# Sinkhorn-sorted attention with a bilinear FFN: output products of two batches and a sixth of batch 0's a, b products by Strassen blocks, in a fixed order of work

## The chip, the cores and the metric

The kernel runs on one core of a Trainium2 chip. The metric is the device time of one execution in microseconds (us), read as the median of several executions. The span in a profile runs from the first to the last instruction and is 1.8 to 2.2 us shorter than the device time. Engines are named as the profile names them: PE is TensorE (matmul), PEld its weight load, DVE is VectorE, ACT is ScalarE, POOL is GpSimd, SP is SyncE; "SPq" is a transfer issued from SP's queue.

## The reference, cut to what matters

```python
def _attn_ref(q, k, v, sort_net):              # q, k, v: 4 x 8 heads x 768 x 64; sort_net: 4 x 8 x 8 x 8
    P = sort_net
    for _ in range(5):                         # Sinkhorn
        P = np.exp(P - np.max(P, axis=-1, keepdims=True))
        P = P / (np.sum(P, axis=-1, keepdims=True) + 1e-09)
        P = P / (np.sum(P, axis=-2, keepdims=True) + 1e-09)
    k_sorted = np.einsum('bhij,bhjcd->bhicd', P, k_b)      # mixes the 8 blocks of 96 tokens
    v_sorted = np.einsum('bhij,bhjcd->bhicd', P, v_b)
    ...                                        # softmax attention inside each block of 96 tokens
def _moe_ref(x, w_a, w_b, w_out):              # x: 3072 x 512; w_a, w_b: 512 x 1536; w_out: 1536 x 512
    return (x @ w_a) * (x @ w_b) @ w_out
```

## The kernel before: the parts that matter

The kernel describes its work as a list of pieces (`add(engine, duration, function, deps, ...)`). A planner, run while the kernel is built, gives each piece a time and an engine by a greedy rule; then the instructions are emitted once, engine by engine, in the order of the plan. The emitted program holds, for each engine, that order and the semaphores to wait for, and no times.

Heads are worked on in *pairs*, four for each batch. The *spread* (`s_all<-mask,p_col`) writes the Sinkhorn result out as blocks for PE; a *mix* is a PE product of `s_all` with k or v. A *plain* product is one without Strassen blocks. *Warm-up* products (`warm_sb`; in the changed kernel `ps<-ws_b`) compute nothing that is used; they keep PE busy in the first 34 us.

The a, b products of batches 1 to 3 use Strassen blocks: seven block products for eight, at the price of sums of weight blocks (`ws_a`, `ws_b`, "w sums", 16 in all, done once) and of activation blocks (`tx`, "x sums", four for each batch). In this kernel all 16 go to GpSimd:

```python
    def w_sums(rank):
        oks = {}
        al = (("POOL", 1.75),)                       # engine and assumed us
        for n, w_sb, ws in (("a", w_a_sb, ws_a), ("b", w_b_sb, ws_b)):
            for c in range(2):
                ... # [cut: slices of w_sb and of ws]
                    op = add(al, None, None, dj, rank=rank)
                    op.fn = lambda ...: tt(op.eng, s[j], x, y, o)   # tensor_tensor

    last = o_p                                       # Sinkhorn, all 32 (batch, head) rows at once
    for it in range(5):
        ... # [cut: exp on ACT; on DVE row sum, reciprocal, p_nat *= 1/row, column sum, reciprocal, p_nat *= 1/column]

    def v_out(b, p):                                 # sorted v leaves to DRAM in one layout ...
        nc.sync.dma_start(out=vdram[b, p], in_=buf(("vb", b, p))...)
    def v_back(b, p):                                # ... and comes back in another, as vs
        nc.sync.dma_start(out=buf(("vs", b, p))[:, :, 2:2 + 2 * D], in_=_ap(vd, 0, ...))
```

The softmax here doesn't subtract the row's maximum and nothing guards it: scores larger than these inputs give would overflow.

## Time and profile before

The median is 245.03 us (244.59 to 245.09, four executions).

| | before |
|---|---|
| span, mean granted TensorE clock | 243.3 us, 1.00 |
| PE busy / DVE busy / POOL busy | 233.7 / 150.1 / 119.6 us |
| first plain a, b product | 27.46 us |
| start of the last matmul | 238.3 us |
| the 16 w sums on GpSimd | between 29 and 71 us, 1.65 us each |

The page's busy table of the kernel before, engine by engine (busy us, share of the span, instructions):

```profile
PE 233.7 (96%) x2204; PEld 132.4 (54%) x2204; DVE 150.1 (62%) x348; ACT 125.3 (52%) x243; POOL 119.6 (49%) x132
```

PE is the limit. The waits view of the kernel before, PE only (line, what it waited for, us in total, times, longest), shows what little it loses:

```profile
engine line waited for: us in total, times, longest us
PE ps L983 <- DVE warm_sb L326: 1.3, 1, 1.3
PE ps L473 <- DMA q<-in_q_dram: 1.1, 2, 0.6
PE ps L500 <- issue: 1.0, 1, 1.0
PE ps L593 <- ACT eT L583: 0.8, 1, 0.8
```

Two stretches of the kernel before, from the busy table by stretch (busy us and, in brackets, instructions of each engine; then clock, DMA share and GB/s):

```profile
core 0: us, PE busy (x) PEld busy (x) DVE busy (x) ACT busy (x) POOL busy (x), PEclk, DMA share, GB/s
50.00:60.00 10.00, 10.00 (x148) 6.75 (x144) 5.41 (x11) 7.66 (x13) 9.96 (x9) 1.00 1.24 194
60.00:70.00 10.00, 10.00 (x126) 6.14 (x124) 6.46 (x12) 5.99 (x10) 9.96 (x10) 1.00 1.00 148
```

Groups of w sums in the kernel before (count, busy us, mean ns, idle time before):

```profile
L306 POOL TENSOR_TENSOR ws_b<-w_b_sb 128x768 bf16<-128x768 bf16 x4 | 6.6, 1648 | 0.0
```

### The profile page before, as it was taken

The page shows a single profiled execution, that of the slowest core. Times are in us where ns is not written, and L with a number is a line of the kernel's source. Part 1 is how long each engine was busy: PE and PEld are TensorE (multiplying, and loading weights), DVE is VectorE, ACT ScalarE, POOL GpSimd, SP SyncE. Part 2 cuts the span into 40 slices and gives each one's busy share as a digit, 9 for nine tenths or more (in the row PEclk, how much of TensorE's full clock was granted, in tenths as well). Part 3 has the DMA queues.
Part 4 walks back from the last instruction along what each step waited for, and adds up shares of the span by engine and source line. Part 5 has one row for each costly group of instructions (what it writes and reads, how often), then busy time and mean ns, then how long its engine had stood idle before and what let it go on. Part 6 is the DMA issues. An engine that isn't in the chain of part 4 may idle for free.

```text
span 243.3 us, 5723 instructions
## 1 busy us (share of the span) xinstructions
PE 233.7 (96%) x2204; PEld 132.4 (54%) x2204; DVE 150.1 (62%) x348; ACT 125.3 (52%) x243; POOL 119.6 (49%) x132
## 2 busy tenths in 40 slices
PE   6998999999989999999999999999999999999992
PEld 2466766666655554665544455665654455565440
DVE  6656654654555738589987452988862448886210
ACT  3366646468655533667654443766631076673100
POOL 8979999999970020069755110173540007355000
PEclk9999999999999999999999999999999999999999
DMA  5999999999965683619998867200035450000135
GB/s 67 180 203 187 202 203 187 167 191 178 162 134 107 167 184 78 149 16 154 135 175 110 192 174 178 46 0 0 3 66 108 96 122 0 1 0 3 43 86 129
DMA packets 50106, 27.90 MB, mean 115 GB/s; under 512 B 28832, under 2 KB 47008, under 8 KB 50080
## 3 DMA queue, kind: packets, MB, share of 16 engines
q0 software_dynamic: 24112, 14.16, 43.3%
q1 hardware_dynamic: 25968, 13.38, 25.7%
q8 instruction: 17, 0.28, 0.5%
q14 instruction: 9, 0.07, 0.1%
HBM read 30.29 MB, written 8.26 MB: 158 GB/s over the span
## 4 chain that ended last, share of the span: by engine, by line
PE 67%; ACT 1%; DVE 1%; issue 0%; ACTq 0%; DVEq 0%
PE ps L831 33%; PE ps L899 26%; PE ps L593 2%; PE ps L578 2%; PE ps L489 1%; PE ps L537 1%; PE ps L473 1%; PE ps L749 1%; ACT f L840 0%; DVE xp L604 0%; ACT o L248 0%; DVE a L306 0%; DVE rec L599 0%; ACTq L840 0%; DVEq L306 0%
## 5 line engine op out<-in xcount | busy, mean ns | idle before, releaser
L306 POOL TENSOR_TENSOR hT<-a,f 128x384 bf16<-128x384 bf16 x39 | 35.5, 918 | 78.1 <-DVE f L306 56.3
L899 PE MATMUL ps<-w_out_sb,hT 128*128 128x512 bf16 x288 | 66.4, 379 | 0.0
L840 ACT COPY f<-ps 128x384 f32<-128x384 f32 x108 | 48.2, 482 | 23.6 <-PE ps L831 21.1
L899 PEld LDWEIGHTS <-hT 128*128 128x128 bf16 x288 | 27.0, 98 | 30.1
L306 DVE TENSOR_TENSOR a<-f,ps 128x384 bf16<-128x384 f32 x54 | 29.4, 549 | 10.4 <-PE ps L831 6.4
L306 DVE TENSOR_TENSOR f<-f,ps 128x384 f32<-128x384 f32 x54 | 28.9, 550 | 8.9 <-PE ps L831 6.0
L583 ACT ACTIVATE eT<-ps 96x768 bf16<-96x768 f32 x32 | 24.9, 806 | 17.2 <-PE ps L578 16.9
L306 DVE TENSOR_TENSOR hT<-a,ps 128x384 bf16<-128x384 bf16 x42 | 23.1, 551 | 12.4 <-PE ps L749 6.9
L248 ACT COPY o<-ps 128x512 f32<-128x512 f32 x15 | 8.8, 585 | 36.3 <-PE ps L899 36.3
L831 PE MATMUL ps<-tx,ws_a 128*128 128x384 bf16 x108 | 25.2, 326 | 0.2 <-ACT f L840 0.2
L831 PE MATMUL ps<-tx,ws_b 128*128 128x384 bf16 x108 | 24.9, 326 | 0.3 <-ACT f L840 0.3
L604 DVE TENSOR_TENSOR xp<-ps,rec 96x512 bf16<-96x512 f32 x32 | 21.4, 677 | 0.4
L749 PE MATMUL ps<-xT,w_a_sb 128*128 128x384 bf16 x96 | 19.6, 327 | 0.0
L749 PE MATMUL ps<-xT,w_b_sb 128*128 128x384 bf16 x96 | 19.6, 326 | 0.0
L831 PEld LDWEIGHTS <-ws_b 128*128 128x128 bf16 x144 | 13.8, 98 | 10.1 <-ACT f L840 0.9
L755 ACT CAST a<-ps 128x384 bf16<-128x384 f32 x24 | 11.5, 479 | 14.9 <-PE ps L749 9.1
L250 DVE COPY o<-ps 128x512 f32<-128x512 f32 x9 | 6.2, 691 | 20.8 <-PE ps L899 20.7
L831 PEld LDWEIGHTS <-ws_a 128*128 128x128 bf16 x144 | 13.5, 98 | 10.1 <-ACT f L840 1.4
L831 PE MATMUL ps<-xT,w_b_sb 128*128 128x384 bf16 x72 | 17.6, 326 | 0.3 <-DVE xp L604 0.2
L831 PE MATMUL ps<-xT,w_a_sb 128*128 128x384 bf16 x72 | 17.5, 326 | 0.0
L831 PEld LDWEIGHTS <-w_b_sb 128*128 128x128 bf16 x108 | 10.4, 98 | 7.9 <-DVE xp L604 0.7
L831 PEld LDWEIGHTS <-w_a_sb 128*128 128x128 bf16 x108 | 10.3, 98 | 7.9 <-ACT f L840 0.6
(90 smaller groups left out, 337.9 us busy)
## 6 DMA issues: line engine op xcount, KB each, us to landing
out_dram<-o SPq DMA_DIRECT2D x48, 128.0 KB, 2.4
k<-in_k_dram POOLq DMA_DIRECT2D x16, 192.0 KB, 6.1
v<-in_v_dram POOLq DMA_DIRECT2D x16, 192.0 KB, 6.1
vd<-vm SPq DMA_DIRECT2D x10, 192.0 KB, 2.9
vs<-vd SPq DMA_DIRECT2D x10, 192.0 KB, 3.1
q<-in_q_dram POOLq DMA_DIRECT2D x16, 96.0 KB, 6.9
w_a_sb<-in_moe_w_a_dram POOLq DMA_DIRECT2D x4, 384.0 KB, 7.1
w_b_sb<-in_moe_w_b_dram POOLq DMA_DIRECT2D x4, 384.0 KB, 9.0
```

Source lines behind the costliest of these rows:

```text
L248: nc.scalar.copy(out=out, in_=in_)
L250: eng.tensor_copy(out=out, in_=in_)
L306: ENG[eng].tensor_tensor(out=out, in0=in0, in1=in1, op=op)
L578: nc.tensor.matmul(sc[:, e, i * BLK:(i + 1) * BLK], lhsT=kT[e * D:(e + 1) * D, at:at + P], rhs=rhs, start=True, stop=True)
L583: nc.scalar.activation(out=buf(("eT", b, p, h))[:, :, 0:HB], in_=buf(("sc", b, p, h))[0:BLK, :, 0:HB], func=AF.Exp, scale=float(scale))
L593: nc.tensor.matmul(ops_[:, e, i * OW:(i + 1) * OW], lhsT=eT[:, e, i * BLK:i * BLK + P], rhs=vs[:, h * NBH + i, e * OW:(e + 1) * OW], start ...
L604: nc.vector.tensor_tensor(out=_ap(xp, h * NBH * 2 * D, [[NB * 2 * D, BLK], [D, 2], [2 * D, NBH], [1, D]]), in0=_ap(ops_, 2, [[1024, BLK], ...
L749: nc.tensor.matmul(pf[:, 0:HW], lhsT=w_sb[:, kc, m * P:(m + 1) * P], rhs=buf(("xT", b))[:, kc, t * HW:(t + 1) * HW], start=(kc == 0), stop ...
L755: ea = add("ACT", 0.48, lambda: nc.scalar.copy(out=buf(("a", b, t, m)), in_=buf(("pf", b, t, m, "a"))[:, 0:HW]), [pa], get=[("a", ("a", b, ...
L831: nc.tensor.matmul(buf(key)[:, 0:HW], lhsT=lf(j), rhs=rf(j), start=start and j == 0, stop=j == 1, skip_group_check=not start)
L840: return add("ACT", 0.48, lambda: nc.scalar.copy(out=buf((name, b, g, n)), in_=buf(kA)[:, 0:HW]), [dep], get=[("f", (name, b, g, n))], rank=r)
L899: nc.tensor.matmul(po, lhsT=hT[:, t * 2 + m // G, m % G, c * P:(c + 1) * P], rhs=w_out_sb[:, m, :], start=(m == 0), stop=(m == KO - 1), sk ...
```

## The change

It is meant to take work off PE and to start PE's products sooner:

- output products of batches 2 and 3 by Strassen blocks (252 products of 256 columns for 144 of 512), with 48 more sums of activations ("S sums") and 8 of weights;
- one sixth of batch 0's a, b products by Strassen blocks too, which needs batch 0's x sums and the w sums early;
- batch 0's Sinkhorn alone first, in another layout with small matmuls; that of batches 1 to 3 later, beside other work;
- w chunks loaded in the order 0, 2, 1, 3, and seven of the 16 w sums on VectorE;
- the order of all pieces from a fixed list in place of the greedy rule; in the plan, sums on GpSimd and VectorE that carry a `port` mark may not overlap.

```diff
+RATE = 365e3
+ORDER = ( b"-b&,###'#+#7#)... [cut: 37 lines, one choice of piece and engine for each two bytes]" )
-STRASSEN_OUT = ()
+STRASSEN_OUT = (2, 3)
+PLAIN_G = 5
...
+        def begin(op, e, w):                        # plan only: marked sums don't overlap
+            return max(at[e], w, port) if e in op.port else max(at[e], w)
...
-    for c in range(1, 4):
+    for c in (2, 1, 3):
         load_ab(c)
...
-        al = (("POOL", 1.75),)
-        for n, w_sb, ws in (("a", w_a_sb, ws_a), ("b", w_b_sb, ws_b)):
-            for c in range(2):
+        for c in (1, 0):
+            al = (("POOL", 1.75), ("DVE", 0.55)) if c == 1 else (("POOL", 1.75),)
+            for n, w_sb, ws in (("a", w_a_sb, ws_a), ("b", w_b_sb, ws_b)):
...
-                    op = add(al, None, None, dj, rank=rank)
+                    op = add(al, None, None, dj, rank=rank - 30.0 * c, port=("POOL", "DVE"))
...
+    if PLAIN_G < G:
+        tx_ok = x_sums(0, R0 + 30.0)
+        for g in range(PLAIN_G, G):
+            ab_strassen(0, g, R0 + 48.0 + 2.0 * (g - PLAIN_G), ws_ok, tx_ok, [])
... [cut: o_sums and out_strassen (about 145 lines), batch 0's Sinkhorn by matmuls, the planner's bookkeeping]
```

## The prediction

> **What bounds it.** TensorE. The page's busy table has PE at 233.7 us of a 243.3 us span; in the busy table by stretch PE is full from 27.46 us (first plain a,b product) to 238.7 us (0.96 us idle), granted clock 1.00. The tail is 4.6 us (last eviction 0.59, then the store). In the timeline, steps from matmul start to start are 163 ns (384 columns) and 216 ns (512): columns/2.4 GHz + 2.5 ns, as the Trainium skill says ("TensorE: Matmul & The Clock Gate", section "Wait — 56ns, not 53.3ns?"); they agree. Estimate for 256 columns: 109 ns; its 98 ns weight load should hide, as 128-column products step at 56 ns.
>
> **Before the first plain product.** Of the first 27.5 us, PE's real work is about 12.2 us (counts x mean step); the rest is warm-up and waits. The Sinkhorn chain (five iterations of 1.76 us, 2.29 to 11.05 us), copies and a spread queued behind warm-up matmuls put the first mix at 14.4 us; the first half of batch-0 attention then takes 13 us.
>
> **What the change does to PE work** (counts from the two instruction orders):
> - Output of batches 2 and 3 by Strassen: 144 x 216 ns = 31.2 us becomes 252 x 109 ns = 27.5 us: -3.7 us.
> - Batch 0: 32 plain products of 384 columns become 28: -0.65 us.
> - Batch-0 Sinkhorn by matmuls: six small f32 products, about +1.5 us (guess), where PE waits anyway.
>
> Added elsewhere: 48 S sums (DVE 0.33 estimated from 0.55 for 768 columns, POOL 0.92), 8 W sums, 4 x sums, more ACT snapshots. In the a,b stages DVE is 85% and POOL 42% busy, so these fit: a few tenths of us of new PE waits. The order is now a fixed list, so waits at 70.9 us (0.8 us) and in the batch-1 Strassen stage (0.3 us each) may go.
>
> **The start.** Only batch 0's Sinkhorn precedes the first mix: 1.6 us + 4 x about 1.45 us (ACT 0.26, PE, three DVE ops, hops) + 1 us: first mix near 11 us, not 14.4. But k of pair 3 now comes after w chunk 0 and two more q halves: 2.9 MB into SBUF; at before's landing rate, near 20.5 us (v of pair 3 landed at 15.5). About 5 us of attention follow: first plain product at about 25.7 us, with 14.6 us of real work done against 12.2. That gains about 1.8 + 2.4 - 1.5 = 2.7 us.
>
> **Tail.** Last piece is 256 columns (0.42 for 0.59-0.69 us), its two stores go to two queues: -0.5 us.
>
> **Sum.** 245.0 - 4.3 (products) - 2.7 (start) - 0.5 (tail) - 0.9 (fewer waits of the search) = 236.6 us. Range 233.8 to 239.6. Faster by over 2% (under 240.1): 0.92; within 2%: 0.07; slower: 0.01.
>
> **What would show each step.** 256-column steps at 109 ns; first mix at 10.5 to 11.5 us; PE waiting for k of pair 3 near 20 us; the last matmul at about 231 us; PE idle under 2 us between; output stages of batches 2 and 3 near 14 us instead of 15.9.
>
> **What would make it wrong.** The 256-column products bound by weight loads (+2 to 3 us); S sums on a slow POOL holding up the output stage (1 to 3 us each); DVE and POOL slowing each other; weight chunks late for the fixed order, stalling PE at 26 to 45 us; the other way, k landing earlier (-1.5 us).

## More of the kernel before

*Held* means that an instruction lasts longer than the shortest one of its form.

A w sum adds or subtracts two SBUF operands of 128x768.

All loads from the inputs are issued by GpSimd (`nc.gpsimd.dma_start`, they convert float32 to bfloat16); the read-back `vs<-vd` and the stores go out on SP's queue. So GpSimd has two jobs: issuing loads, and sums.

In the rounds of the later experiments this kernel's median was 245.1 to 245.6 us.

## The result

The changed kernel is correct and takes 262.25 us median (258.2 to 265.62, four executions); the ratio to the kernel before is 1.061 (95% interval 1.049 to 1.074). All ratios here are the mean time of one kernel's executions over that of the other's in the same rounds, so not quite the ratio of the medians quoted. Executions over 1.5% slower than the fastest of the same kernel are left out of the means. The prediction was 236.6 us, and "slower" had been given 0.01. The times of the changed kernel scatter; its profiled execution (265.62 us) is one of the two that count as slow for it, so the profile below overstates the time by some 2%. The clock goes with it, but only roughly: its four executions had mean granted clocks of 0.945, 0.973, 0.979 and 0.957 in the order 265.6, 262.8, 258.2 and 261.7 us. The explanation therefore rests on the experiments' executions, not on this profile alone.

The page's busy table of the changed kernel:

```profile
PE 239.0 (91%) x2306; PEld 147.3 (56%) x2306; DVE 187.3 (71%) x425; ACT 130.7 (50%) x264; POOL 148.4 (56%) x163
```

DVE is 37 us busier and POOL 29 us. PE's own busy time should have fallen by some 4 us and has risen. The waits view of the changed kernel, PE:

```profile
PE ps L900 <- DVE hT L392: 8.8, 2, 7.9
PE ps L743 <- DMA vs<-vd: 4.6, 1, 4.6
PE ps L650 <- DMA v<-in_v_dram: 2.1, 1, 2.1
PE ps L1292 <- DVE ws_b L414: 1.3, 1, 1.3
PE ps L728 <- DVE rec L749: 1.0, 1, 1.0
```

Three large waits are new: 7.9 us for a VectorE product, 4.6 us for the read-back of v, 2.1 us for a load of v (the 1.3 us on `ws_b` is the start of the warm-up, as before). Stretches of the changed kernel (columns as before):

```profile
20.00:30.00 10.00, 10.00 (x183) 7.90 (x180) 6.70 (x16) 6.01 (x11) 8.89 (x9) 0.50 1.32 204
50.00:60.00 10.00, 8.84 (x114) 5.66 (x112) 9.17 (x12) 5.59 (x9) 9.99 (x10) 1.00 0.90 117
60.00:70.00 10.00, 3.27 (x17) 1.75 (x18) 7.56 (x6) 0.48 (x2) 9.98 (x10) 0.69 1.09 157
110.00:120.00 10.00, 6.99 (x60) 3.65 (x61) 5.47 (x12) 2.78 (x5) 8.39 (x10) 1.00 1.13 207
120.00:130.00 10.00, 8.46 (x55) 5.02 (x55) 5.17 (x11) 4.49 (x10) 3.98 (x5) 0.83 1.94 163
```

In 60 to 70 us PE works 3.3 of 10 us, where it was full before; and the granted clock (PEclk) is 0.50 in 20 to 30 us, after the wait for v, and below 1 again after each of the other long waits. Where the clock was 0.50 the 384-column products stepped at 320 ns (34.6 to 36.2 us), where it was 1.00 at 163 ns; that is how busy time can rise while work does not.

**Who made PE wait 7.9 us?** The timeline of VectorE in the changed kernel in that stretch (start us, duration us, engine, line, operation):

```profile
55.56 1.71 DVE L392 TENSOR_TENSOR tx<-xT 128x768 bf16<-128x768 bf16 x1
57.19 3.00 DVE L392 TENSOR_TENSOR ws_b<-ws_b,w_b_sb 128x768 bf16<-128x768 bf16 x1
60.12 1.98 DVE L392 TENSOR_TENSOR tx<-xT,tx 128x768 bf16<-128x768 bf16 x1
62.02 4.18 DVE L392 TENSOR_TENSOR ws_b<-w_b_sb,ws_b 128x768 bf16<-128x768 bf16 x1
66.13 0.54 DVE L392 TENSOR_TENSOR hT<-a,ps 128x384 bf16<-128x384 bf16 x1
```

The timeline of GpSimd in the same stretch, cut:

```profile
58.09 1.67 POOL L392 TENSOR_TENSOR ws_b<-w_b_sb 128x768 bf16<-128x768 bf16 x1
59.69 1.99 POOL L392 TENSOR_TENSOR ws_a<-ws_a,w_a_sb 128x768 bf16<-128x768 bf16 x1
...
62.39 1.65 POOL L392 TENSOR_TENSOR ws_a<-w_a_sb,ws_a 128x768 bf16<-128x768 bf16 x1
63.97 0.74 POOL L462 DMA_DIRECT2D k<-in_k_dram  x1
```

And PE's timeline, with the wait in brackets:

```profile
66.73 1.14 PE L900 MATMUL ps<-xT,w_a_sb 128*128 128x384 bf16 x3 [7.88 <-DVE hT L392]
```

A 128x768 sum on VectorE took 0.55 us in the kernel before. Here four of them take 1.71, 3.00, 1.98 and 4.18 us, 10.9 us in place of 2.2. The product `hT` that PE waits for (it reads, and so frees, a PSUM bank) is a 0.54 us instruction queued behind them; it runs at 66.13 us and PE goes on at 66.73 us. Each of the four overlaps sums or load issues of GpSimd. VectorE's held time in the first 75 us is 14.3 us (21 instructions), against 0.01 us before. Small instructions suffer as much as large ones; the groups view of the changed kernel has batches 1 to 3's Sinkhorn product at a mean of 1359 ns, where the shortest took 202 ns:

```profile
L568 DVE TENSOR_TENSOR p_nat<-p_nat,csum 24x64 f32<-24x64 f32 x4 | 5.4, 1359 | 0.0
```

**The 4.6 us for `vs<-vd`.** PE's timeline, SP's queue and GpSimd's queue in the changed kernel:

```profile
121.54 0.90 PE L743 MATMUL ps<-vs,eT 96*128 96x66 bf16 x16 [4.56 <-DMA vs<-vd]
112.25 0.49 SPq L700 DMA_DIRECT2D vs<-vd  x1
111.51 0.76 POOL L462 DMA_DIRECT2D k<-in_k_dram  x1
112.26 0.72 POOL L462 DMA_DIRECT2D v<-in_v_dram  x1
112.97 1.46 POOL L462 DMA_DIRECT2D k<-in_k_dram  x2
```

The last read-back of batch 2 is issued at 112.25 us and lets PE go on at 121.54 us, 9.3 us later (its landing itself is not in the trace); those others of this kernel whose landing is recorded took 2.6 to 4.4 us from their issue. What differs is that GpSimd had begun at 111.51 us to issue the loads of batch 3 (its first k lands 7.0 us after its issue), and, as I read it, that PE had run out of other work.

The theories to test: **(A)** everything follows from the early wait for v of pair 3 and the half clock behind it, which makes the fixed order run late and then collide; **(B)** the sums on GpSimd and VectorE hold each other by themselves, whatever the start does; **(C)** the read-back against batch 3's loads is a cost of its own; and **(D)** the fixed list is a bad order, and the greedy rule would have been better. (The expectations of e1 and e2 were written with other letters: their "theory C" is that the half clock comes from thin PE activity at the start and not from the wait for v.)

### The profile page after: what moved, and what is told of

Its sections match the earlier page's. It is cut to its first block, busy times and chain, and to the rows that moved or that the text cites. A ratio compares the mean times of both kernels' runs of the same rounds, so it can differ in the third digit from the quotient of the medians.

```text
span 263.5 us, 6046 instructions
## 1 busy us (share of the span) xinstructions
PE 239.0 (91%) x2306; PEld 147.3 (56%) x2306; DVE 187.3 (71%) x425; ACT 130.7 (50%) x264; POOL 148.4 (56%) x163
## 4 chain that ended last, share of the span: by engine, by line
PE 75%; DVE 10%; DMA 8%; POOL 3%; issue 2%; ACT 0%; DVEq 0%; SPq 0%; ACTq 0%
PE ps L983 32%; PE ps L1053 10%; PE ps L1146 9%; PE ps L900 9%; DMA vs<-vd 4%; DMA v<-in_v_dram 3%; PE ps L743 3%; PE ps L728 3%; DVE ws_b L392 3%; PE ps L639 2%; DVE hT L392 2%; PE ps L650 2%; PE ps L623 2%; PE ps L687 1%; DMA vd<-vm 1%
## 5 line engine op out<-in xcount | busy, mean ns | idle before, releaser
L992 ACT COPY f<-ps 128x384 f32<-128x384 f32 x114 | 51.0, 483 | 39.6 <-PE ps L983 36.9
L392 POOL TENSOR_TENSOR hT<-a,f 128x384 bf16<-128x384 bf16 x44 | 40.6, 935 | 37.8 <-DVE f L392 18.5
L1053 PE MATMUL ps<-w_out_sb,hT 128*128 128x512 bf16 x144 | 35.1, 380 | 0.0
L983 PEld LDWEIGHTS <-ws_b 128*128 128x128 bf16 x152 | 14.4, 98 | 10.0 <-ACT f L992 0.6
L1053 PEld LDWEIGHTS <-hT 128*128 128x128 bf16 x144 | 12.7, 98 | 13.0 <-DVE xp L754 0.2
L983 PE MATMUL ps<-xT,w_b_sb 128*128 128x384 bf16 x76 | 19.1, 337 | 0.0
L392 POOL TENSOR_TENSOR tx<-xT 128x768 bf16<-128x768 bf16 x4 | 6.9, 1735 | 21.5 <-DMA xT<-xp 21.5
L743 PE MATMUL ps<-vs,eT 96*128 96x66 bf16 x256 | 14.1, 204 | 4.6 <-DMA vs<-vd 4.6
L322 ACT CAST kT<-ps 128x768 bf16<-128x768 f32 (+1 forms) x17 | 11.9, 706 | 11.7 <-PE ps L639 10.2
L743 PEld LDWEIGHTS <-eT 96*128 96x128 bf16 x256 | 12.2, 104 | 9.7 <-issue 5.6
L749 DVE RECIPROCAL rec<-ps 96x8 f32<-96x8 f32 x32 | 6.1, 196 | 15.9 <-PE ps L743 15.7
```

The source lines that it names most:

```text
L322: nc.scalar.copy(out=out, in_=in_)
L392: ENG[eng].tensor_tensor(out=out, in0=in0, in1=in1, op=op)
L743: nc.tensor.matmul(ops_[:, e, i * OW:(i + 1) * OW], lhsT=eT[:, e, i * BLK:i * BLK + P], rhs=vs[:, h * NBH + i, e * OW:(e + 1) * OW], start ...
L983: nc.tensor.matmul(buf(key)[:, 0:HW], lhsT=lf(j), rhs=rf(j), start=start and j == 0, stop=j == 1, skip_group_check=not start)
L992: return add("ACT", 0.48, lambda: nc.scalar.copy(out=buf((name, b, g, n)), in_=buf(kA)[:, 0:HW]), [dep], get=[("f", (name, b, g, n))], rank=r)
L1053: nc.tensor.matmul(po, lhsT=hT[:, t * 2 + m // G, m % G, c * P:(c + 1) * P], rhs=w_out_sb[:, m, :], start=(m == 0), stop=(m == KO - 1), sk ...
```

## The experiments

Each is the changed kernel with one edit unless said otherwise. "Held" is VectorE's held time in the first 75 us. The experiments were run in four jobs on different chips, so across jobs compare the ratios. The change's ratio rests on two fast executions (interval 1.049 to 1.074); by it, e5 gives back 0.047 (about 11 us; with both intervals 8 to 15) and e6 0.030 (about 7 us; 4 to 11).

| run | median us (range) | ratio to before | held us |
|---|---|---|---|
| before | 245.03 (244.6 to 245.1) | 1 | 0.01 |
| the change | 262.25 (258.2 to 265.6) | 1.061 | 14.3 |
| e1: v of pair 3 first | 264.38 (261.9 to 267.2) | 1.070 | 13.9 |
| e2: warm-up in the wait | 266.05 (261.7 to 267.1) | 1.075 | 15.8 |
| e3: greedy rule | 266.37 (265.4 to 270.6) | 1.085 | 9.7 |
| e4: all w sums on GpSimd | 262.67 (262.0 to 265.1) | 1.070 | 15.9 |
| e5: all w sums on VectorE | 249.89 (249.1 to 253.7) | 1.015 | 2.3 |
| e6: batch 3's loads gated | 253.83 (253.4 to 258.9) | 1.031 | 12.7 |
| e7: e1 + e5 + e6 | 242.00 (241.7 to 242.3) | 0.984 | 2.5 |
| e8: greedy + e5 + e6 | 260.41 (259.9 to 260.8) | 1.058 | 6.4 |
| e9: e5 + e6 | 242.67 (242.3 to 245.1) | 0.991 | 2.3 |
| b1: before, 8 w sums on VectorE | 246.93 (246.5 to 248.5) | 1.005 | 6.3 |
| e7 again | 242.58 (242.3 to 243.2) | 0.989 | 2.3 |
| e9 again | 242.72 (241.6 to 243.3) | 0.990 | 2.3 |

### e1: v of pair 3 ahead of the first w_a chunk

```diff
+        for x, y in ((33, 35), (34, 36)):      # swap issue and transfer in the decoded list
+            i, j = [n for n, o in enumerate(order) if o // 2 in (x, y)]
+            order[i], order[j] = order[j], order[i]
```

> Edit: in the fixed list, v of pair 3 of batch 0 is loaded before the first w_a chunk, not behind it. Nothing else moves. Theory A (cascade: the 2.1 us wait for v of pair 3 at 15.8 us halves the granted clock of TensorE to 36 us, this makes PE late, and late PE throws the VectorE and GpSimd pieces of the list onto each other): v lands near 14.5 us, no wait there, clock 1.00 from 20 to 36 us, first plain product near 27 us in place of 34.3, the 7.9 us wait at 58 us gone or under 2 us, about 243 us. Theory B (VectorE sums collide with GpSimd by themselves, whatever PE does): the start gains 2 to 8 us, but waits of over 5 us stay between 40 and 70 us; about 252 us. Theory C (the halved clock comes from thin PE activity in the start and not from that wait): clock still about 0.5 from 20 to 36 us.

Measured: 264.38 us. The wait for v is gone and the clock is full where it was half:

```profile
20.00:30.00 10.00, 8.71 (x199) 6.22 (x191) 7.61 (x21) 6.45 (x13) 8.98 (x10) 1.00 1.31 203
```

But the 7.9 us wait is still there (now at 53 us), the read-back's wait is 6.7 us, and the held time is 13.9 us. So theory A falls: with the start mended, the holding and the read-back cost as much as before. The 252 us that was expected under theory B did not come either: the first plain product was 5.7 us earlier than in the change's profile (28.56 us), and the end was no earlier.

### e2: warm-up columns in the wait

```diff
+            if o.seq == 177:                   # the first product that reads v of pair 3
+                cols = 4700
```

> Edit: 2.0 us of warm-up matmuls go just ahead of the first product with v of pair 3, so PE is busy while it waits for it; the wait itself stays. If the idle time halves the clock (theory A): the mix still starts near 18 us, but the clock stays 1.00 to 36 us, the first plain product comes near 29.5 us, 5 us earlier than in the changed kernel. If it is the lateness alone that counts, or thin activity later (theory C): the clock is still about 0.5 from 20 to 36 us and the time is within 2 us of the changed kernel's 258 to 266.

Measured: 266.05 us; waits of 3.6 us (behind a held Sinkhorn product), 7.9 us and 4.8 us. But the edit had nothing to cover, so e2 does not test whether an idle PE halves the clock: the early wait is not a regular thing. The v of pair 3 landed at 16.6 us here, and at 16.4 to 16.6 us in five more profiled executions with the change's order of loads (e4, e5, e6 and twice e9), against 18.05 us in the profiled execution of the change. The wait of 2.1 us belongs to that one execution. The half clock does not need it: in the profiles of e4 and e5, without that wait, the clock was 0.50 from 28 to 32 us, and in e2 from 32 to 36 us, after the wait of 3.6 us. In e6, e7 and the first e9 it was full from 20 to 40 us, in the second e9 0.67 from 28 to 32 us. What sets it stays open; thin PE activity is not ruled out.

### e3: the greedy rule in place of the list

```diff
-ORDER = ( b"-b&,###'... " )
+ORDER = b""
```

> Edit: the fixed list is emptied, so the kernel's own greedy rule orders the same pieces of work; all else of the change stays. If the list is what costs (it was made for landings that do not happen, and all engines' order follows it): faster than the changed kernel, 240 to 250 us. If the added work itself costs (Strassen sums on VectorE and GpSimd, the shared access to SBUF): no faster than 255 us, with VectorE sums of over 1.5 us in the trace.

Measured: 266.37 us, a little slower than with the list. Theory D falls. VectorE is held here too, partly later, where the new sums of the output stage (they lie in buffers named `k` and `v`) cost PE 3.9 us in the waits view; the longest waits in sum are again for the read-back (5.9 us). The list is the better order of the two; neither avoids the holding.

### e4 and e5: where the w sums run

```diff
-  op.fn = lambda ...: tt(op.eng, s[j], x, y, o)
+  op.fn = lambda ...: tt("POOL", s[j], x, y, o)     # e4: the seven of VectorE on GpSimd too
+  op.fn = lambda ...: tt("DVE", s[j], x, y, o)      # e5: all sixteen on VectorE
```

> Edit: the seven w sums that the list gives to VectorE are issued on GpSimd, at the same place of the list. If VectorE is held by GpSimd (a VectorE sum of two SBUF inputs waits while GpSimd runs one): no VectorE sum of over 1.5 us is left of the w sums, the 7.9 us wait of PE at 58 us falls under 3 us although GpSimd has 12 us more to do; 252 to 257 us. If PE's wait came from its own lateness or from weights landing late: it stays over 5 us and GpSimd's extra work makes the time no better than 258 us.

> Edit: all sixteen w sums are issued on VectorE, at their places of the fixed list; GpSimd then runs no sum of two SBUF inputs before 49 us. VectorE has 9 sums (about 5 us of work) more. If VectorE's long sums are waits for a GpSimd sum that runs at the same time (lock theory): none of the p_nat products and w or x sums between 20 and 70 us takes over 1.5 us but those beside the three s_all products, and the 7.9 us wait of PE falls under 3 us: 250 to 256 us. If those ops are long for another reason (their own load, or GpSimd's issuing of loads): VectorE stays late, with 5 us more to do, and the time is 262 us or more.

Measured: e4 262.67 us, e5 249.89 us. With all sums on GpSimd, VectorE's own share of the work falls, the 7.9 us wait falls to 2.9 us, and yet the kernel stays as slow: now the Sinkhorn products and the x sums are held (held time 15.9 us), and PE waits 4.0 us at 37 us. One Sinkhorn product of 0.20 us lasts 5.99 us there, from 34.49 us, while GpSimd runs three w sums with loads between and after them: the longest holding of all runs. From the waits view of e4, PE:

```profile
PE ps L900 <- ACT a L906: 4.0, 1, 4.0
PE ps L900 <- DVE hT L392: 3.3, 2, 2.9
```

With all sums on VectorE, which gives it nine more (an estimate of 5 us *more* work at 0.55 us each), the kernel is about 11 us faster and the 7.9 us wait is gone, although the profiled execution of e5 is a slow one. The longest wait in e5's waits view, PE, is now

```profile
PE ps L743 <- DMA vs<-vd: 6.4, 1, 6.4
```

That GpSimd sums at all in this stretch is the cost, not VectorE's load. It also tells why the kernel before was free of it with all 16 sums on GpSimd: its Sinkhorn ended at 11 us, before GpSimd's first sum, and its x sums came after the last; the change moved both into GpSimd's stretch of sums.

e5 kept the read-back's wait, so that is not a consequence of the late sums.

### e6: batch 3's loads wait for batch 2's read-backs

GpSimd copies one element of each `vs` tile of batch 2 ahead of its first load of batch 3, so those loads are issued only when the read-backs have landed.

```diff
+        def gate():
+            if b == 3 and not gated:
+                gated.append(1)
+                for n in range(HP):
+                    nc.gpsimd.tensor_copy(out=gate_sb[0:1, n:n + 1], in_=buf(("vs", 2, n))[0:1, 0, 2:3])
```

> Edit: ahead of the first load for batch 3, GpSimd copies one element of each v tile of batch 2, so these loads wait until batch 2's v has come back. If the 4.6 us (here 4.6 to 6.7) wait of PE near 111 to 117 us comes from that round trip sharing the DMA engines with the loads of batch 3: the return takes about 3 us in place of 9, the wait falls under 1.5 us and the time falls by 3 to 6 us against the changed kernel (258 to 266). If the round trip is late because of PE and VectorE alone, the wait stays at 4 us or more.

Measured: 253.83 us, about 7 us faster than the change by the ratios (3 to 6 were expected). GpSimd's timeline shows the gate's last copy waiting for the read-back instead of PE:

```profile
110.47 0.18 POOL L504 COPY gate_sb<-vs 1x1 bf16<-1x1 bf16 x1 [4.40 <-DMA vs<-vd]
```

That read-back was issued at 106.46 us and landed about 4.0 us later, not 9.3. PE has no `vs<-vd` wait in this run; the 7.9 us wait stays, as the longest of e6's waits view:

```profile
PE ps L906 <- DVE hT L393: 9.3, 2, 7.9
```

So theory C holds. It isn't only batch 3's loads: in e4 a read-back issued at 83.49 us, with the loads issued from 77 to 82 us still in flight, took 8.1 us.

### e7 and e9: the three edits together, and without e1's

> Edit: v of pair 3 ahead of the first w_a chunk, all w sums on VectorE, and the loads of batch 3 gated, together. If the waits measured (about 2 us at the start, 8 us at 55 us, 5 us at 115 us, and the half-rate clock that follows each) are separate costs on the path of PE, they add: 243 to 249 us. If PE's waits only move (the list is too tight for any landing or sum that is late): 255 us or more.

> The changed kernel with all sixteen sums of the weight chunks on VectorE and with GpSimd gated behind the read-back of batch 2, but with the list's own order of loads (the first w_a chunk ahead of v of pair 3). If the two costs (sums held by GpSimd about 12 us, the read-back about 8 us) simply add and the early wait for v of pair 3 with the half-rate clock after it costs nothing in the end, it is at about 242 us like the version with all three. If the early wait is a cost of its own once the other two are gone, it is 2 to 8 us slower than that version, 244 to 250 us, with a wait of about 2 us near 16 us and a granted clock near 0.5 from 20 to 30 us.

Measured: e7 242.00 us and e9 242.67 us. The costs add, as far as the intervals tell: e5 takes 0.047 off the ratio and e6 0.030, from 1.061 leaves 0.984; e9 has 0.991 and 0.990, e7 0.984 and 0.989. Both are far faster than the change, but only about 1% faster than the kernel before: their intervals (0.978 to 0.996 over the four) exclude 1, and at the 2% that a verdict asks for they count as the same or unclear. The longest PE wait of e7 is the one at the start of the warm-up:

```profile
PE ps L1301 <- DVE ws_b L418: 1.3, 1, 1.3
```

The page's busy table of e7:

```profile
PE 228.7 (95%) x2294; PEld 142.0 (59%) x2306; DVE 178.2 (74%) x434; ACT 130.2 (54%) x264; POOL 134.1 (56%) x158
```

PE's busy time is 5.0 us below that of the kernel before, at a granted clock of 0.997 (12 matmul records are missing, and 3.0 us of the difference are fewer warm-up products). The Sinkhorn product of the groups view is back at its own length:

```profile
L577 DVE TENSOR_TENSOR p_nat<-p_nat,csum 24x64 f32<-24x64 f32 x4 | 0.8, 204 | 0.0
```

To see whether e1's edit is worth anything, both were run again on one chip in the same rounds:

> The version with all three edits once more, beside the one without the reordered load, on one chip and in the same rounds. If the early wait for v of pair 3 costs something once the other two costs are gone, this one is at least 0.5% faster than the other; if it costs nothing, they agree within 0.4%. Its ratio to before should be 0.980 to 0.989 again.

> The version with the sums on VectorE and the gate, but the list's own order of loads. About 242 to 243 us, ratio to before 0.984 to 0.993; the difference to the version with all three in these rounds tells what the early wait is worth, which the first look put at 0.7 us across two jobs.

Measured: 242.58 and 242.72 us, a difference of 0.06%, within what the rounds tell apart. So e1's edit is worth nothing that they can show (under 0.4%). The wait of about 2 us that was expected of e9 did not come in either run (0.4 and 0.5 us at 16.6 us): v landed in time.

### e8: greedy rule with e5 and e6

The load rate that the planner assumes is lowered to 320e3 as well (365e3 in the change, 333e3 in the kernel before), and w sums have VectorE as their one engine.

> Edit: no fixed list; the greedy rule, with all w sums on VectorE only, a load rate of 320 in place of 365 thousand bytes per us in the plan (nearer to the landings seen), and the gated loads of batch 3. If collisions of VectorE with GpSimd and late landings explain the greedy version's loss (266 us): 244 to 252 us. If the Strassen sums of the output stage cost as much as they save: over 252 us with waits of PE of 5 us in sum after 195 us.

Measured: 260.41 us. With the greedy rule other sums collide: PE waits 3.2 us at 50 us behind VectorE's w sums beside GpSimd's spread (`s_all`), and 3.4 us and several of 0.9 us behind the S sums of the output stage (7.2 us in sum from 192 us on). The 244 to 252 us were missed, and the other branch came. So the list is worth about 17 us over the greedy rule once the w sums are off GpSimd (e9 has the same two edits; the two differ in the assumed load rate as well).

### b1: the kernel before with one part of the change

```diff
+                al = (("POOL", 1.75), ("DVE", 0.55)) if c == 1 else (("POOL", 1.75),)
```

> The kernel before with one part of the change alone: the eight sums of chunk 1 of each weight may run on VectorE or GpSimd as its own planner picks (in the changed kernel the list gave VectorE seven). If sums on VectorE beside GpSimd's sums are the cost whatever else changes, VectorE's two-SBUF-input sums show an excess of 3 to 15 us over their shortest form (0.16 us in all before), and the kernel is 1 to 8 us slower than before, unless its planner gives VectorE none of them. If the excess needs the change's other parts (the batches' Sinkhorn products and the S sums), it stays within 1% of before and the excess is under 2 us.

Measured: 246.93 us (ratio 1.0048, interval 1.0004 to 1.0092). Its planner gave VectorE all eight. They are held 6.3 us in sum and make PE wait 2.2 and 1.8 us; the kernel ends about 1.6 us slower. So the holding needs no other part of the change, but, as I read the waits, it is dear only when VectorE's queue has what PE waits for.

### m1 and m2: the holding by itself

Two micro kernels (one execution each) with phases separated by ScalarE. Their outputs are wrong, which doesn't matter for the times. VectorE sums two 128x768 SBUF operands; GpSimd does what the phase says.

> Micro benchmark, wrong result on purpose, eight fenced phases. One VectorE sum of two 128x768 SBUF operands alone takes about 0.50 us, one on GpSimd alone about 1.65 us. If the two engines exclude each other for a whole instruction, then eight VectorE sums beside four GpSimd sums show single VectorE sums of 1.6 to 4 us, and the phase lasts about as long as the two alone added, near 10.6 us. If GpSimd issuing loads also holds VectorE, the phases with six loads show VectorE sums of over 1 us beside the loads; if only its sums do, they stay at 0.50 us. VectorE sums with one PSUM operand, and copies, beside GpSimd sums, and VectorE sums beside GpSimd memsets, stay at their lengths alone if only a second SBUF input on both engines collides.

VectorE's and GpSimd's timelines in m1, cut to the phases that matter (in order: alone; beside four GpSimd sums, with those sums; beside load issues alone; with one PSUM operand beside GpSimd sums, 128x384; the first eight of 16 copies beside GpSimd sums, the view ends at 93 us):

```profile
17.71 4.71 DVE L40 TENSOR_TENSOR d_out<-src 128x768 bf16<-128x768 bf16 x8 [3.00 <-ACT src L36]
35.27 9.95 DVE L40 TENSOR_TENSOR d_out<-src 128x768 bf16<-128x768 bf16 x8 [12.85 <-ACT src L36]
35.38 7.65 POOL L52 TENSOR_TENSOR p_out<-src 128x768 bf16<-128x768 bf16 x4 [3.02 <-ACT src L36]
48.28 4.71 DVE L40 TENSOR_TENSOR d_out<-src 128x768 bf16<-128x768 bf16 x8 [3.06 <-ACT src L36]
66.31 7.03 DVE L44 TENSOR_TENSOR d_out<-src,ps 128x384 bf16<-128x384 bf16 x12 [3.06 <-ACT src L36]
84.68 8.37 DVE L48 COPY d_out<-src 128x768 bf16<-128x768 bf16 x8 [3.57 <-ACT src L36]
```

Eight sums alone take 4.71 us (0.56 us each). Beside four GpSimd sums they take 9.95 us: four of them last 1.87 us, one for each GpSimd sum, and four 0.56. GpSimd's sums stretch from 1.63 us alone to 1.83 to 1.94 us. Here the engines take turns, instruction by instruction, and VectorE's held sum ends 0.4 us after GpSimd's. Beside one GpSimd sum followed by five loads, one of ten VectorE sums lasts 1.87 us and the others 0.56. Load issues with no sum in GpSimd's queue cost nothing (4.71 us again), nor do GpSimd memsets (4.71 us), nor sums with one PSUM operand (12 in 7.03 us, 0.55 us each, no longer than in the kernels). A bfloat16 SBUF-to-SBUF copy, which has one SBUF input, is held just the same, against the expectation: four of the 16 last 1.67 us, the others 0.36 us.

This is what the Trainium skill says ("SBUF — State Buffer", section "Who interferes with whom"): the two engines share a pair of ports under an exclusive lock, a VectorE instruction with two SBUF inputs contends with a GpSimd instruction that reads SBUF, and whichever comes second "fully blocks". Runs agree, with 1.87 us for 0.56.

In the changed kernel some instructions stayed held longer than one sum: 4.18 us at 62.02 us, though GpSimd's sum had ended at 64.04 us and only load issues followed. m2 has GpSimd's queue as sum, three loads, sum, three loads, sum.

> Micro benchmark, wrong result on purpose. GpSimd's queue is sum, three loads, sum, three loads, sum, as in the changed kernel; VectorE runs sums of the weight chunks' own strided form, back to back, then with one PSUM copy between, then with two. In the changed kernel some VectorE sums stayed held for one or two load issues after a GpSimd sum had ended. If load issues between sums keep the hold, single VectorE sums here last 2.5 to 4.5 us; if not, no VectorE sum lasts longer than one GpSimd sum and its own time, about 1.9 to 2.4 us, and those beside load issues stay at 0.55 us.

VectorE and GpSimd in m2's phase with one PSUM copy between VectorE's sums, from the timeline, in order of time, cut (`ws` and `wp` are the sums, `ld` the loads):

```profile
44.29 1.94 POOL L91 TENSOR_TENSOR wp<-w 128x768 bf16<-128x768 bf16 x1 [8.42 <-ACT w L81]
...
46.18 2.16 POOL L65 DMA_DIRECT2D ld<-in_k_dram  x3
...
47.04 1.51 DVE L85 TENSOR_TENSOR ws<-w 128x768 bf16<-128x768 bf16 x1
48.36 1.67 POOL L91 TENSOR_TENSOR wp<-w 128x768 bf16<-128x768 bf16 x1
```

The sum at 47.04 us is held for 1.51 us although from 46.18 to 48.34 us GpSimd only issues loads: its one sum ended at 46.23 us and the next begins at 48.36 us. In all of m2's phases VectorE gets one sum through about every 1.9 us until GpSimd's last sum is over, and then runs at 0.56 us again. So loads issued *between* sums hold VectorE as the sums do; loads with no sum behind them don't (m1). No single sum lasted over 1.98 us here, so the expected 2.5 us and more did not come: this accounts for the holding past the end of a sum, but the single instructions of 3.00 and 4.18 us, and e4's of 5.99 us, are not reproduced. Nor is it a full rule: in e9 VectorE's sums at 44.22 and 44.69 us kept their 0.55 us beside two loads that stood between two `s_all` products of GpSimd. Why one kind of queue holds and the other not stays open.

## Why the prediction was wrong, point by point

**What PE saves: right for the products, about half right for their stages.** Steps of the 256-column products, start to start, have a median of 109 ns in the trace, as estimated (the rule of the Trainium skill that the prediction cites agrees), and their weight loads hide. At that step 252 of them take 27.5 us, for the 31.1 us of 144 products of 512 columns. But the stages gave back less. From the first to the last output product, less the a, b products that stand between (163 ns each), batches 2 and 3 take 15.3 us each in the kernel before, and 13.7 and 14.9 us in e7: 2.1 us less in sum, not 3.7. Batch 3's stage has three gaps, 1.2 us together, before products that wait for VectorE; in e9's trace of that stage an S sum of 0.35 us lasts 1.06 us beside one of GpSimd (at 224.68 us). So "S sums holding up the output stage", one of the prediction's risks, came in once, at its lower end. From the first plain product to the start of the last matmul e7 takes 206.7 us for 210.8 before, 4.1 us less.

**The failed step: "In the a,b stages DVE is 85% and POOL 42% busy, so these fit: a few tenths of us of new PE waits."** It judged the sums by each engine's share of time. Two faults were in that. The harm came at 28 to 66 us, where GpSimd was already busy for 43.8 of 44.9 us in the kernel before (27.46 to 72.40 us, busy table by stretch), from w sums, batch 0's x sums and the Sinkhorn products, not in the later a,b stages whose shares it looked at. And VectorE and GpSimd are not two resources for such sums: they take turns, so that a 0.56 us (or 0.20 us) instruction lasts 1.9 us and more, up to 5.99. The term measures about 11 us: that is what e5 gives back (ratio 1.061 to 1.015), of which 7.9 us is one PE wait; the rest is, as I read the waits views, smaller waits and slower clocks after them, but no run splits it further. "DVE and POOL slowing each other" stood among the risks, but without a size, and the page that sizes it was not used.

**Not foreseen: the read-back of batch 2 against batch 3's loads.** The prediction had no term for it. It measures about 7 us (e6: ratio 1.061 to 1.031), a PE wait of 4.6 us and the clock after it. The kernel before loads batch 3 as well, but in its profile every read-back landed 2.6 to 3.5 us after its issue.

**The start: partly right, and worth nothing by itself.** The first mix came at 12.3 us (predicted 11, before 14.4), and k of pair 3 landed at 21.3 us (predicted 20.5). But the first plain product came at 34.27 us, not 25.7. Part of that is this execution's late v and its half clock; yet even in e7, with neither, it comes at 28.24 us, 0.8 us later than before. The term that was mis-sized is "about 5 us of attention follow": in e7 k of pair 3 lands at 20.78 us, and 7.5 us follow.

**The fixed list: right in kind.** Fewer waits than with the greedy rule were predicted (0.9 us). e8 against e9 has about 17 us between the two once the w sums are off GpSimd; with the sums as the change has them (against e3) it is about 4 to 6 us.

**What remains.** e7 at 242.0 us is still 5.4 us above the prediction. From its profiled execution: the first plain product comes 2.5 us later than predicted (28.24 for 25.7), the stretch from there to the last matmul is 206.7 us for about 205.3 (+1.4), and the tail after the start of the last matmul is 4.9 us, as long as before (5.0), where the prediction's own numbers (last matmul at about 231, a span of about 234.8) leave 3.8 us (+1.1). So the start was over-valued by 2.5 us, and the stretch and the tail together by 2.5; how these last divide rests on "about 231". By its own term the tail was to be 0.5 us shorter; it is 0.1 shorter. VectorE is still held for 8.6 us after 75 us in e7 (0.16 us in the whole trace of the kernel before), where GpSimd still has sums and products; what that costs beyond the gaps named above was not tested.

## What to carry to other kernels

Before spreading element-wise sums over VectorE and GpSimd, ask how many inputs each reads from SBUF (a bfloat16 SBUF copy with one was held too, m1): two engines that take turns are one resource, and the free share of each means nothing. Put all two-SBUF-input work of a stretch on VectorE and leave GpSimd the loads (0.56 us for 1.65 us, and about 11 us in the end), and remember that moving *other* VectorE work beside GpSimd's sums is as bad as moving the sums (e4). When prefetched loads and a small transfer that the limiting engine needs soon go out together, hold the prefetch back until the small one has landed (e6).

## What the Trainium skill lacked or had wrong

- "SBUF — State Buffer", section "Who interferes with whom": right about the exclusive turn (1.87 us for a VectorE sum of 0.56 us; copies 1.67 for 0.36), and it gives as inferred that `tensor_tensor` does not contend with the writing of descriptors. Load issues alone indeed cost nothing (m1: eight sums in 4.71 us with and without them). It lacks that load issues between two GpSimd sums can hold VectorE as well (m2: 1.51 us for a sum of 0.54 us beside load issues alone), and that they didn't between two `s_all` products (e9).
- The same section lacks what both sides lose when both keep issuing such sums: in m1 GpSimd's took 1.83 to 1.94 us beside VectorE's, 1.63 us alone, while VectorE's took 1.87 for 0.56. It also lacks how one short instruction can stay held over several GpSimd sums (e4: 5.99 us for 0.20).
- "TensorE: Matmul & The Clock Gate", section "What's actually happening": it has half rate follow an idle window of about 3.4 us, and full rate about 3.4 us of sustained work. In the profiled execution of the change a wait of 2.1 us, with short gaps before it, was followed by a clock of 0.50 from 20 to 36 us, with PE recorded as at work nearly all the while (one more wait of 1.0 us); in e6, without that wait, the clock was full in that stretch, but in e4 and e5, also without it, it was 0.50 from 28 to 32 us.
- The same page, section "Back-to-back issue gap": it gives about 131 ns for a sustained 512-column product and about 81 ns at 128 columns; the steps here are 216 ns and 56 ns, that is, the formula it reserves for isolated products.
- "DMA: Bandwidth & Descriptors", section "Queues, rings and completion order": it says that each DMA engine goes round the queue rows packet by packet, and gives no figure for what that does to a small transfer. Here a 192 KB read-back took 9.3 us with a batch's loads in flight (8.1 us in e4), and 2.6 to 4.4 us otherwise in the profile of the change.
